# When the last group's first weight slabs are asked for, and when the sums that make them pause

## The chip, the cores and the metric

The kernel runs on one core of one Trainium2 chip. The metric is device time in microseconds (us), from the start to the end of the kernel on the device. Five engines work side by side, each in its own order: TensorE multiplies matrices (PE in the profile, its weight loads PEld), VectorE (DVE), ScalarE (ACT) and GpSimd (POOL) do elementwise work, and SyncE (SP) issues nearly all of this kernel's DMAs. [...]

## The reference

Two blocks follow each other: attention within chunks of 64 tokens, and a Fourier mix with a two-layer network behind it. All is in 32-bit floats; the two network weights come as 64-bit floats.

```
scores = q_c @ k_c.T / sqrt(64)                 # 8 batches, 8 heads, 9 chunks of 64 tokens
out    = softmax(scores) @ v_c
x      = out, heads side by side                # (8, 576, 512)
u      = x + real(fft(fft(x, axis=1), axis=2))
un     = (u - mean(u)) / sqrt(var(u) + 1e-6)    # over the last axis
result = u + relu(un @ w_ch1) @ w_ch2           # 512 -> 2048 -> 512
```

## The kernel before

**Groups and steps.** The 4,608 tokens are 36 tiles of 128 rows; four tiles are a group, and there are nine groups, numbered 0 to 8 (`NG` is 9). Group g is the four large tiles of batch g, for g up to 7; group 8 is the four tiles of "rest" rows, left over from pairs of batches. The network of a group is a Python generator, `mlp(g)`, that yields after each step. The main loop at the end of the kernel runs the generators one after the other, counts the steps in `t`, and after each step lets other work go on: attention and Fourier mix of later batches, and the weight work below. `begin[g]` is the step count at which group g begins. Group 6 begins at 182, group 7 (`NG - 2`) at 212, group 8 (`FEW`) at 242. The order of every engine's instructions is the order in which this loop writes them.

**Products.** From group 2 on, the first layer is done in `up_halves`: each pair of row blocks takes seven products instead of eight, with combined weights that were stored to DRAM in `s1`. There are four pairs, so 28 products of 16 PE instructions each (L1262). From group 1 to group 7 the second layer is done in `down_halves`, with seven products and combined weights from `s2` (L1313). In group 8 alone it is done in `down_few`, which takes 26 products for a 4 by 2 blocking (L1377); its weights are blocks from `s2` and sums of them, in `s3`.

**Slabs.** Weights are fetched by `fetch(which)`, which issues one request on SP. `fetch(1)` (L1135) brings a 256 KB slab of `s1` into one of ten places in `wa`; it is called after each up product, for the product ten later, and waits until PE has finished with the place. `fetch(2)` (L1140) brings a 1 MB slab of `s2` into one of three places in `wb`, after each of the seven down products. `fetch(3)` (L1138) brings a 512 KB slab for one of the 26 products; there are eleven places, six in the space of `wb` that `down_halves` has left, and five (`more`) in tiles that are free by then. Its first eleven requests are made by the main loop, the others by `down_few` after each product.

**Weight sums.** The blocks in `s3` are made once, by the generator `make_rest`. It works in two halves; in each it loads eight blocks (L1104), makes 23 sums or differences on POOL (L1113, `MADE`), and stores 19 of them (L1120), each store three stored sums behind the sum that was just made. It has 14 half-block buffers, so that some sums wait until an earlier store has left its buffer. It yields after every second sum, and between the loads. The main loop starts it at step 202 (`ready_at[NG - 3]`), in group 6, and steps it once a step from 207 on; it is done at step 233, in the down phase of group 7.

**Other work on POOL.** In the up phases it makes operands (L1149), in `down_halves` four sums after the second product (L1345) and parts of the output after the third and fourth (L1350, L1325, L1326); in group 8 it makes operands for `down_few` (L1163). The outputs go out on SP (L1027, L1036).

## Time and profile before

| | |
|---|---|
| median of three runs | 1081.1 us (1078.39, 1081.1, 1081.45) |
| profiled execution | 1078.96 us, span 1076.9 us |
| PE busy, PE weight loads busy | 1053.0 us (98%), 837.3 us (78%) |
| DVE, POOL, ACT busy | 585.0 us (54%), 406.1 us (38%), 310.3 us (29%) |
| DMA | 212.71 MB, mean 198 GB/s |
| granted TensorE clock | 0.998 |

All of the profile's times count from the start of the span. Group 7 runs its up products from 875.3 and its down products from 925.3, group 8 its up products from 975.3 and its 26 products from 1026.3. Rows of PE's timeline overlap a little[...]: a row's start is better for measuring pace than its length. In a row of the windows, the stretch is followed by its length, and by the busy time and number of instructions of PE, PEld, DVE, ACT and POOL; then come the granted clock, DMA's busy share, and GB/s. In a row of a timeline, start and length are followed by engine, line, operation, output and inputs, and the number of instructions; idle time before it, and what ended it, stand in brackets.

### The profile page before, as it was taken

How to read it: one execution, taken by the hardware profiler on the slowest of the kernel's cores; microseconds unless marked ns; L12 is line 12 of the kernel's file. 1: busy time of each engine (PE TensorE's matmuls, PEld its weight loads, DVE VectorE, ACT ScalarE, POOL GpSimd, SP SyncE). 2: the span in 40 equal slices, each digit the busy share in tenths (PEclk: the TensorE clock that was granted, in tenths of full speed). 3: DMA queues.
4: the chain of work that ended last, by engine and by line, in shares of the span. 5: the costliest groups of instructions: out<-in, count | busy, mean ns of one | idle time of the engine just before them, and what ended most of it. 6: DMA issues, size and time to landing. Idle time of an engine off the chain costs nothing.

```text
span 1076.9 us, 19916 instructions
## 1 busy us (share of the span) xinstructions
PE 1053.0 (98%) x7402; PEld 837.3 (78%) x7402; DVE 585.0 (54%) x1271; ACT 310.3 (29%) x730; POOL 406.1 (38%) x531
## 2 busy tenths in 40 slices
PE   8999989999999999999999999999999999999997
PEld 6645445446888888888888888888888888888786
DVE  4898985324567465664565554745564435433331
ACT  4688563212113411322032312331233012101200
POOL 4311017573515140344134321624061837850281
PEclk9999999999999999999999999999999999999999
DMA  8767466598467546883678256945653569957563
GB/s 176 240 184 214 122 190 210 162 299 292 153 193 224 161 155 181 231 238 118 189 210 229 99 183 199 260 129 189 208 158 110 196 211 317 337 174 241 186 225 107
DMA packets 159293, 212.71 MB, mean 198 GB/s; under 512 B 69308, under 2 KB 106172, under 8 KB 152926
## 3 DMA queue, kind: packets, MB, share of 16 engines
q1 hardware_dynamic: 155548, 208.04, 63.0%
q10 hardware_dynamic: 3330, 2.76, 1.1%
q8 instruction: 59, 0.97, 0.4%
q0 software_dynamic: 320, 0.66, 0.3%
q14 instruction: 36, 0.29, 0.1%
HBM read 177.31 MB, written 34.08 MB: 196 GB/s over the span
## 4 chain that ended last, share of the span: by engine, by line
PE 77%; DMA 6%; DVE 5%; issue 3%; POOL 3%; ACT 3%; SPq 3%; POOLq 0%; DVEq 0%; ACTq 0%
PE pb L1313 18%; PE pa L1262 16%; PE pa L1313 14%; PE pb L1262 12%; PE dn L1377 4%; PE up L1195 2%; PE pt L397 2%; DMA xall<-in_moe_w_ch_dram 2%; PE mix L838 2%; DMA wa<-s 2%; PE z L719 1%; PE xp L498 1%; SPq L263 1%; PE up L1175 1%; PE sc L448 1%
## 5 line engine op out<-in xcount | busy, mean ns | idle before, releaser
L1262 PE MATMUL pa<-unT,wa 128*128 128x256 f32 x672 | 159.9, 381 | 1.6 <-DVE wa L1270 1.6
L1262 PEld LDWEIGHTS pa<-unT,wa 128*128 128x128 f32 x672 | 126.3, 190 | 19.5 <-DVE wa L1270 2.1
L1262 PE MATMUL pb<-wa 128*128 128x256 f32 x448 | 106.7, 381 | 2.6 <-DMA wa<-s 2.6
L1313 PE MATMUL pa<-wb,h 128*128 128x256 f32 x448 | 101.5, 380 | 0.0
L1313 PE MATMUL pb<-wb,h 128*128 128x256 f32 x448 | 100.7, 379 | 0.0
L1262 PEld LDWEIGHTS pb<-wa 128*128 128x128 f32 x448 | 84.2, 190 | 14.8 <-issue 2.8
L1313 PEld LDWEIGHTS pa<-wb,h 128*128 128x128 f32 x448 | 83.9, 190 | 11.3
L1313 PEld LDWEIGHTS pb<-wb,h 128*128 128x128 f32 x448 | 84.1, 190 | 10.9
L1149 POOL TENSOR_TENSOR h<-h 128x256 f32<-128x256 f32 x56 | 47.0, 850 | 96.2 <-DVE wb L1147 93.4
L555 POOL COPY xall<-xall 1x512 f32<-1x512 f32 x28 | 17.8, 636 | 147.9 <-DVE xall L515 120.4
L1268 DVE TENSOR_TENSOR wa<-pb,wa 128x256 f32<-128x256 f32 x56 | 23.7, 424 | 73.0 <-ACT wa L1267 73.0
L1216 PE MATMUL dn<-wb,h 128*128 128x512 f32 x128 | 58.9, 609 | 0.0
L1267 ACT COPY wa<-pa 128x256 f32<-128x256 f32 x56 | 20.8, 372 | 126.8 <-PE pa L1262 126.8
L1195 PE MATMUL up<-unT,wa 128*128 128x512 f32 x128 | 56.8, 596 | 0.0
L1262 PE MATMUL pa<-wa 128*128 128x256 f32 x224 | 53.9, 384 | 0.8 <-DMA wa<-s 0.8
L1262 PE MATMUL pb<-unT,wa 128*128 128x256 f32 x224 | 53.0, 379 | 0.0
L1313 PE MATMUL pb<-wb,yall 128*128 128x256 f32 x224 | 51.2, 382 | 0.0
L1313 PE MATMUL pb<-wb 128*128 128x256 f32 x224 | 50.7, 379 | 0.0
L1313 PE MATMUL pa<-wb,yall 128*128 128x256 f32 x224 | 50.5, 379 | 0.0
L1276 ACT ACTIVATE h<-pa 128x256 f32<-128x256 f32 x56 | 21.5, 383 | 100.7 <-PE pa L1262 99.8
L1175 PE MATMUL up<-unT,wa 128*128 128x512 f32 x108 | 49.4, 598 | 0.0
L1262 PEld LDWEIGHTS pa<-wa 128*128 128x128 f32 x224 | 41.7, 190 | 7.2 <-ACT wa L1267 1.1
(287 smaller groups left out, 1955.7 us busy)
## 6 DMA issues: line engine op xcount, KB each, us to landing
wb<-s SPq DMA_DIRECT2D x49, 1024.0 KB
wa<-s SPq DMA_DIRECT2D x196, 256.0 KB
xall<-in_moe_w_ch_dram SPq DMA_DIRECT2D x22, 512.0 KB
q<-in_q_dram SPq DMA_DIRECT2D x96, 112.0 KB
k<-in_k_dram SPq DMA_DIRECT2D x96, 112.0 KB
wb<-s SPq DMA_DIRECT2D x16, 512.0 KB
v<-in_v_dram SPq DMA_DIRECT2D x124, 64.0 KB
s<-part SPq DMA_DIRECT2D x30, 256.0 KB
```

The lines of the kernel that those rows point to most:

```text
L397: nc.tensor.transpose(pt[:, j, :], src(j), ident)
L838: nc.tensor.matmul(out=mix[:, cols], lhsT=zt[:, T], rhs=tab, start=(T == 0), stop=(T == 3), skip_group_check=True,)
L1149: nc.gpsimd.tensor_tensor(out=h1[:, m, hi], in0=h1[:, m, lo], in1=h1[:, m, hi], op=ALU.subtract)
L1175: nc.tensor.matmul(out=up, lhsT=w1[:, kk, m * 128:(m + 1) * 128], rhs=unT[:, kk], start=(kk == 0), stop=(kk == KD - 1), skip_group_check=True,
L1195: nc.tensor.matmul(out=up, lhsT=w1[:, kk, m * 128:(m + 1) * 128], rhs=unT[:, kk], start=(kk == 0), stop=(kk == KD - 1),)
L1216: nc.tensor.matmul(out=dn, lhsT=h1[:, m, s * 128:(s + 1) * 128], rhs=w2[:, m, :], start=(m == 0), stop=(m == KF - 1),)
L1262: nc.tensor.matmul(out=dst, lhsT=w[:, kk, r], rhs=rhs[o][:, kk], start=(o in (0, 1) and kk == 0), stop=(kk == 1), skip_group_check=True,)
L1267: nc.scalar.copy(a, dst)
L1268: nc.vector.tensor_tensor(out=b, in0=pbs[r][:, 0], in1=a, op=ALU.add)
L1276: nc.scalar.activation(out=h1[:, m, lo], in_=dst, func=ACTF.Relu)
L1313: nc.tensor.matmul(out=dst, lhsT=lhs[:, m], rhs=w[:, m], start=(o in (0, 2) and m == 0), stop=(m == HF - 1), skip_group_check=True,)
L1377: nc.tensor.matmul(out=dst, lhsT=lhs[:, m], rhs=w[:, m], start=(fresh and not half and m == 0), stop=(m == 3), skip_group_check=True,)
```

## The change

Two places in the main loop change. `make_rest` is no longer stepped at steps 215, 219, 223, 227, 231, 235 and 239, that is, at every fourth step from the beginning of group 7; its 28 stretches end at step 240 instead of 233. The eleven first `fetch(3)` requests of group 8 are no longer all made at step 244, but one at each of the steps 244 to 254; the places for them are set up at step 244 as before.

```diff
                 if t == ready_at[NG - 3]:
                     rest_ = make_rest()
                     next(rest_)
-                if t > ready_at[NG - 3] + 4:
+                if t > ready_at[NG - 3] + 4 and (t < begin[NG - 2] or t % 4 != 3):
                     next(rest_, None)
                 if t == begin[FEW] + 2:
                     more = [xall[:, 2 * G:2 * G + 4, :].rearrange("p a f -> p (a f)")[:, i * Z3:(i + 1) * Z3] for i in range(2)]
                     more += [one_p.tile([128, Z3], FP32, tag=tag, name="more") for tag in ("q", "k", "zf")]
                     slab3.extend(a.rearrange("p (m e) -> p m e", m=4) for a in more)
-                    for _ in range(NS3):
-                        fetch(3)
+                if begin[FEW] + 2 <= t < begin[FEW] + 2 + NS3:
+                    fetch(3)
```

The SP requests of that stretch are the same in number and size, in another order. TensorE, VectorE and ScalarE have the same instructions in the same order as before; on POOL, sums of `make_rest` stand later among its other work.

## The prediction

> **What bounds the kernel now.** I read the page first (PE busy 98% of the span, weight loads 78%, the next engine 54%), then PE's waits, the windows of the last two groups, PE's timeline there, the DMA queue's timeline, and POOL's waits. TensorE is the bound, at full granted clock, so a change gains only where PE stands still. The windows are the up and down phases of group 7, then those of group 8:

> ```profile
> 875.28:925.33 50.05, 49.05 (x226) 42.33 (x225) 24.87 (x52) 13.55 (x31) 34.07 (x29) 1.00 0.89 307
> 925.33:975.28 49.95, 49.95 (x241) 43.99 (x241) 15.80 (x30) 2.45 (x6) 31.29 (x29) 1.00 0.61 205
> 975.28:1026.26 50.98, 48.59 (x226) 42.49 (x225) 16.95 (x40) 13.73 (x31) 7.84 (x7) 1.00 0.61 216
> 1026.26:1076.90 50.64, 45.04 (x209) 39.34 (x207) 12.51 (x31) 0.69 (x2) 27.00 (x22) 1.00 0.55 177
> ```

> Length first, then PE's busy time: the two up phases hold 1.00 and 2.39 us of idle PE, the down phases none before the tail. PE's timeline shows where:

> ```profile
> 909.65 1.89 PE L1262 MATMUL pa<-unT,wa 128*128 128x256 f32 x8
> 911.77 1.97 PE L1262 MATMUL pb<-wa 128*128 128x256 f32 x8 [0.23 <-DMA wa<-s]
> 913.57 1.89 PE L1262 MATMUL pa<-unT,wa 128*128 128x256 f32 x8
> 916.23 1.97 PE L1262 MATMUL pa<-wa 128*128 128x256 f32 x8 [0.77 <-DMA wa<-s]
> ...
> 997.71 1.89 PE L1262 MATMUL pa<-unT,wa 128*128 128x256 f32 x8
> 1002.00 1.97 PE L1262 MATMUL pb<-wa 128*128 128x256 f32 x8 [2.39 <-DMA wa<-s]
> ```

> A row is one up product, with one 256 KB slab. From 975.27 to 997.71 thirteen of them start 1.726 us apart; 28 make 48.3 us. Against that pace group 7 loses 1.7 us and group 8 2.7 us: **4.4 us is all there is to gain**. The DMA queue shows why the slabs are late. In group 8:

> ```profile
> 977.19 5.50 SPq L1135 DMA_DIRECT2D wa<-s  x4
> 982.74 3.86 SPq L1138 DMA_DIRECT2D wb<-s  x6
> 986.65 1.21 SPq L1138 DMA_DIRECT2D xall<-s  x2
> 988.13 2.87 SPq L1138 DMA_DIRECT2D more<-s  x3
> 991.97 12.35 SPq L1135 DMA_DIRECT2D wa<-s  x11
> ```

> Eleven 512 KB requests (5.77 MB) stand ahead of the fifth up slab. It is asked for at 991.97 and, by the chain of work, takes 9.89 us: the very slab that PE waits for until 1002.00. DMA moved 402 GB/s from 986 to 996. In group 7 it is the weight sums' stores and loads:

> ```profile
> 898.80 0.90 SPq L1135 DMA_DIRECT2D wa<-s  x2
> 899.81 5.52 SPq L1120 DMA_DIRECT2D s<-part  x4
> 905.42 0.88 SPq L1104 DMA_DIRECT2D part<-s  x2
> 906.41 1.89 SPq L1135 DMA_DIRECT2D wa<-s  x2
> 908.65 0.32 SPq L1104 DMA_DIRECT2D part<-s  x1
> 909.03 0.42 SPq L1104 DMA_DIRECT2D xall<-s  x1
> 909.55 0.44 SPq L1135 DMA_DIRECT2D wa<-s  x1
> ```

> The row at 898.80 ends with the 11th slab request of group 7. Four stores then hold the queue 5.5 us: the last waits for the first half's last sum (POOL, 903.71 to 904.98). So the 12th and 14th requests go out at 906.41 and 909.55, and PE waits for these two, 0.23 and 0.77 us.

> [...]

> **The change part by part.** PE, DVE and ACT have the same instructions in the same order. POOL and SP have the same work reordered.

> *Part 1, one slab a step.* The 11 requests go out at the end of group 8's steps 2 to 12 instead of all at step 2. No byte and no instruction is added. Between two of them now stand one or two up slabs, each tied to PE's pace (3.45 us a step of two products). Demand: 18 up slabs of 256 KB and 11 of 512 KB are 10.5 MB over 48.3 us, 217 GB/s, half of what the burst reached. An up slab then has at most one 512 KB request just ahead, 1.3 us at 402 GB/s; it is requested ten products, 17.3 us, before its use. Even with the slowest landing seen, 9.89 us, it comes in time. Gain: 2.7 us. The other side is lateness: with both stalls gone group 8 starts at 973.6, its 12th step ends 21 products, 36.3 us, later at 1009.9, where the 11th product slab is asked for; its product runs at 973.6 + 48.3 + 10 x 1.73 = 1039.2. That is a cover of 29 us against a landing of 1.3 us (its bytes at 402 GB/s) to 9.9 us (the slowest seen): nothing.

> *Part 2, the pause.* From step 0 of group 7 (212 in the step count) the sums skip every fourth step: they end at step 240 instead of 233, before group 8 starts (242). POOL's sums are 1.30 us each (mean of L1113), 23 in each half. For group 7's up phase: before, 11 slab requests stand ahead of the four stores; after, 14 do. From 887.03 to 899.81 the queue passed 19 requests, 0.67 us each. Counting the new order from the same store at 887.03, the 12th slab request is 19 places on, 899.8, and the 14th 901.1, instead of 906.41 and 909.55. With 6.55 us to land (the chain's figure for the late one) they are there at 906.4 and 907.7; PE wants them at 875.28 + 21 x 1.726 = 911.5 and at 915.0. The next in danger, the 15th, now stands behind the four stores and two loads: sums end about 905, so it goes at 906.3, lands at 912.9, and is wanted at 916.7. The 17th goes where the 14th went, 909.55, lands at 916.1, wanted at 920.2. All have 3.8 us to spare. Gain: 1.7 us. From the 19th on the slabs are for group 8, 50 us away.

> *Where the pushed work goes.* Ten more sums than before fall behind POOL's four L1345 sums of the down phase. These come sooner or at the same time; they wait for PE's second down product, 923.6 + 2 x 6.91 = 937.4, and end at 942.7 (before: 948.8, behind the backlog). Then four sums to 947.9, then L1350 to 949.3 (before: 954.0), which shortens DVE's 5.63 us wait for L1350. The other L1113 sums fit in between and end near 964, with the last four stores behind them. Those stand between group 7's output stores on SP; the ones behind wait for DVE until about 968 anyway, and group 8's first slab request waits for PE at 975.3. On SP, the 1 MB down slabs now have stores ahead of them that wait for POOL: the third one goes when PE releases the buffer at 944.4, its stores needing only a sum ended at 944; before it went at 953.09, behind five stores. The fourth waits for PE at 951.3. No cost.

> *Sum.* -2.7 - 1.7 = -4.4 us at most. [...] I take **-4.2 us**. On the profiled execution (1078.96 us, of which the span is 1076.9): 1074.8, a ratio of 0.9961. That execution lies 0.2% below the median of the runs; the ratio on 1081.1 gives 1076.9.

> **Rivals.**
> 1. *Only the burst's stall goes*, because in group 7 DMA stays full (0.89 busy) and another slab is late in place of the two: the 15th's 3.8 us of slack is the thinnest place. For it: landings there took 5 to 6.6 us and sums could run later than before. Against: three more slab requests are ahead, 5.2 us of PE's work. -2.7 + 0.2: 1078.6.
> 2. *Nothing moves*: the slabs that come late in group 8 are just other ones, or group 7's gain is lost again at the first down slab. Against: 217 GB/s, and 29 us of cover. 1081.
> 3. *Slower*, by a ring between SP and POOL in group 7's down phase: POOL waits for a buffer whose store stands behind a 1 MB request, SP holds this until PE frees its slab, and the third such request stands behind stores of sums not yet made. The trace of before shows the kind: POOL waited 15.53 us for a store, until 875.14, while SP waited for PE's down slabs. The third slab is wanted at 923.6 + 5 x 6.91 = 958.2; 1 MB needs 2.6 us at 402 GB/s and at most 6.7 (asked for at 953.09, used at 959.8), so a request after 951.5 stops PE: POOL has 7 us to lose. A wait of 15.5 us there makes PE late by 8.5, net +4.3: 1085.4. It decides from 11.3 us on. Against: the one sum that needs a store behind such a request (the 13th, its store at about 931) comes after L1345, which holds POOL until 942.7 anyway.

> **How the numbers follow.** A difference under 0.3% (3.2 us) is about what a measurement of this kernel can't tell from none: its three runs span 3.06 us. The forecast -4.2 has 0.62; rival 1 0.19; rival 2 0.08; rival 3 0.11. The forecast lands beyond -0.3% some 8 times in 10 (0.50), rival 1 2 in 10 (0.04): faster 0.54. The rest of these and rival 2 make same 0.35; slower 0.11. Low end: the profiled execution's level less all of 4.4, 1074.5. High end: rival 2 at the highest run, 1081.5. Outside lie rival 3 and some 0.06 of noise. The likeliest case's own range is 1075.4 to 1078.4 (half the runs' spread each way).

> **What would show it.** Right: no PE wait for wa in either up phase, both near 48.3 us; no 400 GB/s stretch in group 8's up phase; L1138 requests single, about 3.5 us apart; sums running on past L1350 to about 964; down phases as long as before. Wrong: a PE wait for wb in group 7's down phase (rival 3), for wa after 911 (rival 1), or for dn's slabs after 1022.

## The result and the profile after

The changed kernel takes 1077.22 us (median of 20 runs, 1074.83 to 1080.25), the kernel before 1080.18 us (20 runs, 1076.95 to 1081.64): ratio 0.9976, with an interval of 0.9967 to 0.9986. That is 2.6 us, inside the predicted range, and a little less than the 0.3% beyond which the prediction counted it as faster. Two repeats further down gave 0.9962 and 0.9969.

The profiled execution took 1076.13 us, its span 1074.1 us. The windows of the changed kernel, again for the up and down phases of group 7 and of group 8 (length, then busy time of PE, PEld, DVE, ACT and POOL, granted clock, DMA share, GB/s):

```profile
876.53:924.89 48.36, 48.36 (x226) 42.59 (x225) 24.13 (x52) 13.57 (x31) 31.05 (x27) 1.00 0.90 318
924.89:975.18 50.29, 50.27 (x241) 44.05 (x241) 18.10 (x30) 2.45 (x6) 34.90 (x31) 1.00 0.62 195
975.18:1023.54 48.36, 48.36 (x226) 42.59 (x225) 16.95 (x40) 13.89 (x31) 8.00 (x7) 1.00 0.65 236
1023.54:1074.10 50.56, 44.90 (x209) 39.20 (x207) 12.51 (x31) 0.54 (x2) 26.85 (x22) 0.97 0.54 177
```

Both up phases are at PE's own pace: 48.36 us with no idle time, where they took 50.05 and 50.98. From first product to first product, group 7's down phase is 0.2 us longer (50.31 against 50.11); the 0.2 us stand in front of one transpose (L397), and the profile does not show what ended that wait. From the start of group 7 to the end of the span the two profiles differ by 4.1 us. They differ by only 2.8 us in the whole span, because this execution came to group 7 1.26 us later (876.38 against 875.12), in a part of the program in which the change has moved nothing.

The DMA queue's timeline of the changed kernel, first where group 7's slabs were late, then at group 8's requests:

```profile
900.61 1.62 SPq L1135 DMA_DIRECT2D wa<-s  x3
902.54 4.04 SPq L1120 DMA_DIRECT2D s<-part  x4
907.00 0.81 SPq L1104 DMA_DIRECT2D part<-s  x2
907.91 0.85 SPq L1135 DMA_DIRECT2D wa<-s  x2
...
989.04 2.05 SPq L1135 DMA_DIRECT2D wa<-s  x2
991.14 0.42 SPq L1138 DMA_DIRECT2D wb<-s  x1
992.50 2.05 SPq L1135 DMA_DIRECT2D wa<-s  x2
994.59 0.42 SPq L1138 DMA_DIRECT2D wb<-s  x1
```

The row at 900.61 holds the 12th to 14th slab requests, now ahead of the four stores. Group 8's product slabs go out one at a time between up slabs, except the last three, which go together at 1006.68. DMA still has a full stretch there, fuller and longer than the 402 GB/s over 10 us of the old burst:

```profile
992.00:1007.00 15.00, 15.00 (x72) 13.20 (x71) 5.58 (x14) 3.61 (x8) 7.48 (x6) 1.00 1.03 409
```

No slab comes late in it: by the updates of the DMA semaphores in the trace, each up slab that group 8 asks for lands at least 5.8 us before its product is due. But one stretch looks worse than before. These are the same queue's last requests of group 7:

```profile
966.15 1.10 SPq L1027 DMA_DIRECT2D out_dram<-wb  x2
968.85 0.81 SPq L1036 DMA_DIRECT2D out_dram<-wb  x2
969.75 5.90 SPq L1120 DMA_DIRECT2D s<-part  x4
975.74 1.08 SPq L1027 DMA_DIRECT2D out_dram<-wb  x2
976.92 1.96 SPq L1036 DMA_DIRECT2D out_dram<-wb  x2
978.98 6.95 SPq L1135 DMA_DIRECT2D wa<-s  x4
985.98 0.42 SPq L1138 DMA_DIRECT2D wb<-s  x1
```

The four last stores of the sums take 5.90 us of the queue, the output stores behind them are late, and group 8's first slab is asked for 3.9 us after the group begins, where it was 1.9 before (977.19 against 975.27). No PE wait comes of it here. What it is worth without the other half of the change is the main finding of the experiments.

### The profile page after: what moved, and what is told of

It reads as the page before. It is cut to its first block, busy times and chain, and to the rows that moved or that the text cites. A ratio compares the mean times of both kernels' runs of the same rounds, so it can differ in the third digit from the quotient of the medians.

```text
span 1074.1 us, 19924 instructions
## 1 busy us (share of the span) xinstructions
PE 1052.4 (98%) x7402; PEld 838.0 (78%) x7402; DVE 586.5 (55%) x1271; ACT 310.6 (29%) x730; POOL 406.8 (38%) x531
## 4 chain that ended last, share of the span: by engine, by line
PE 82%; DMA 5%; DVE 5%; ACT 3%; SPq 3%; issue 1%; POOL 0%; DVEq 0%; ACTq 0%
PE pb L1313 18%; PE pa L1262 18%; PE pa L1313 14%; PE pb L1262 13%; PE dn L1377 4%; PE up L1195 4%; PE pt L397 2%; PE dn L1216 2%; DMA xall<-in_moe_w_ch_dram 2%; PE mix L838 2%; PE z L719 1%; PE xp L498 1%; PE sc L448 1%; SPq L263 1%; DMA out_dram<-o 1%
## 5 line engine op out<-in xcount | busy, mean ns | idle before, releaser
L1262 PE MATMUL pa<-unT,wa 128*128 128x256 f32 x672 | 160.0, 381 | 1.5 <-DVE wa L1270 1.5
L1262 PEld LDWEIGHTS pa<-unT,wa 128*128 128x128 f32 x672 | 126.3, 190 | 19.3 <-DVE wa L1270 2.0
L1262 PE MATMUL pb<-wa 128*128 128x256 f32 x448 | 106.6, 381 | 0.0
L1262 PEld LDWEIGHTS pb<-wa 128*128 128x128 f32 x448 | 84.4, 190 | 11.5
L1262 PE MATMUL pa<-wa 128*128 128x256 f32 x224 | 53.9, 383 | 0.0
L1262 PE MATMUL pb<-unT,wa 128*128 128x256 f32 x224 | 52.9, 379 | 0.0
L1313 PE MATMUL pa<-wb,yall 128*128 128x256 f32 x224 | 50.5, 379 | 0.0
L1175 PE MATMUL up<-unT,wa 128*128 128x512 f32 x108 | 49.4, 598 | 0.0
L855 POOL TENSOR_TENSOR xall<-y,xall 128x513 f32<-128x513 f32 x14 | 21.4, 1526 | 68.4 <-DVE y L849 68.4
```

What stands on the lines that cost most here:

```text
L855: eng.tensor_tensor(out=x[:, 0:w], in0=y[:, 0:w], in1=x[:, 0:w], op=ALU.add)
L1175: nc.tensor.matmul(out=up, lhsT=w1[:, kk, m * 128:(m + 1) * 128], rhs=unT[:, kk], start=(kk == 0), stop=(kk == KD - 1), skip_group_check=True,
L1262: nc.tensor.matmul(out=dst, lhsT=w[:, kk, r], rhs=rhs[o][:, kk], start=(o in (0, 1) and kk == 0), stop=(kk == 1), skip_group_check=True,)
L1313: nc.tensor.matmul(out=dst, lhsT=lhs[:, m], rhs=w[:, m], start=(o in (0, 2) and m == 0), stop=(m == HF - 1), skip_group_check=True,)
```

## The experiments

The theory: what counts is the order of requests on SP. A slab is late when something that waits, or something large, stands ahead of it. In the kernel before, the four stores ahead of group 7's late slabs held the queue 5.5 us (the last waited for a sum that ended at 904.98), the burst ahead of group 8's 9.2 us. Rivals: the change works by moving bytes out of a full stretch; the pause costs something by itself; only one of the two parts does the work.

The table has every run, with the time that the two up phases lost against 48.35 us (the pace), worked out from the starts of the phases' first products on PE's timeline. "Group 8 asks" is the time from the start of the group to its first slab request.

| run | ratio to before, interval | group 7 up lost | group 8 up lost | group 8 asks |
|---|---|---|---|---|
| before, first profile | | 1.70 | 2.63 | 1.9 |
| again_before | 0.9997, 0.9985 to 1.0010 | 1.01 | 4.44 | 1.9 |
| the change, first profile | 0.9976, 0.9967 to 0.9986 | 0 | 0 | 3.9 |
| again_after | 0.9962, 0.9950 to 0.9975 | 0 | 0 | 3.8 |
| after_third | 0.9969, 0.9956 to 0.9983 | 0 | 0 | 3.5 |
| spread_only | 0.9969, 0.9959 to 0.9979 | 1.05 | 0 | 1.9 |
| spread_again | 0.9970, 0.9959 to 0.9981 | 0.33 | 0 | 1.9 |
| pause_only | 1.0045, 1.0026 to 1.0064 | 0.68 | 8.36 | 4.1 |
| pause_no_tail | 0.9997, 0.9983 to 1.0012 | 0 | 4.28 | 1.9 |
| one_pause | 0.9997, 0.9983 to 1.0012 | 0.15 | 4.50 | 1.9 |
| burst_later | 0.9994, 0.9980 to 1.0007 | 0.26 | 1.46 | 1.9 |
| late_burst | 0.9956, 0.9940 to 0.9973 | 0 | 0 | 4.0 |
| one_pause_spread | 0.9964, 0.9951 to 0.9977 | 0 | 0 | 1.9 |
| late_spread | 0.9965, 0.9953 to 0.9976 | 0.48 | 0 | 3.5 |

### Each part alone, and both kernels once more

Part 1 alone is this edit of the kernel before:

```diff
-                    for _ in range(NS3):
-                        fetch(3)
+                if begin[FEW] + 2 <= t < begin[FEW] + 2 + NS3:
+                    fetch(3)
```

> Part 1 alone. Theory: the up slabs of group 8 come in time and nothing else changes: group 8's up phase 48.4 us instead of 51.0, group 7's still about 50 us with PE waits of about 1 us for wa; 2.6 us less than before (-0.24%). Rival, that the whole gain comes from one part: 4.2 us less here and nothing from the pause alone, or the other way round.

As the theory had it: group 8's up phase 48.35 us, group 7's still with a wait for wa, and 0.9969. The gain is 3.4 us where 2.6 was expected; the interval of the ratio, 2.3 to 4.4 us, holds both. The PE timeline's row for group 7's wait, in this kernel:

```profile
916.80 1.97 PE L1262 MATMUL pb<-wa 128*128 128x256 f32 x8 [0.81 <-DMA wa<-s]
```

Part 2 alone:

```diff
-                if t > ready_at[NG - 3] + 4:
+                if t > ready_at[NG - 3] + 4 and (t < begin[NG - 2] or t % 4 != 3):
                     next(rest_, None)
```

> Part 2 alone. Theory: group 7's up phase 48.4 us instead of 50.05, the burst's wait in group 8 stays at 2.4 us; about 1.6 us less than before (-0.15%). Rival, that stores pushed into the down phase cost as much there: group 7's down phase longer than 49.95 us, no gain.

Neither theory nor rival: it is 0.45% (4.9 us) slower than before. The down phase is not to blame (50.24 us, against 50.1); the loss is in group 8's up phase. The DMA queue and PE's timeline of this kernel, and its windows around the wait:

```profile
975.18 5.90 SPq L1120 DMA_DIRECT2D s<-part  x4
981.17 1.09 SPq L1027 DMA_DIRECT2D out_dram<-wb  x2
982.35 2.08 SPq L1036 DMA_DIRECT2D out_dram<-wb  x2
984.52 6.62 SPq L1135 DMA_DIRECT2D wa<-s  x4
991.20 4.08 SPq L1138 DMA_DIRECT2D wb<-s  x6
```
```profile
1002.91 1.89 PE L1262 MATMUL pa<-unT,wa 128*128 128x256 f32 x8
1010.37 3.75 PE L1262 MATMUL pb<-wa 128*128 128x256 f32 x8 [5.57 <-DMA wa<-s]
1013.91 2.70 PE L1262 MATMUL pa<-unT,wa 128*128 128x256 f32 x8
```
```profile
1000.00:1008.00 8.00, 4.80 (x23) 3.88 (x21) 1.78 (x5) 2.86 (x6) 3.65 (x3) 1.00 1.02 418
1008.00:1016.00 8.00, 5.63 (x14) 4.59 (x15) 0.00 (x0) 0.21 (x1) 3.81 (x4) 0.57 0.94 360
```

Two things are added to the old wait. The burst starts 10.7 us after group 8 begins (991.20 against 980.46) instead of 7.5, with the same four slabs ahead of it, and so PE waits 3.2 us longer, 5.57 us. And the product after the wait takes 3.75 us instead of 1.89: the granted clock was 0.57 in that stretch.

> The kernel before, once more. If the two waits for slabs are fixed by the order of requests, this profile shows them again within 0.3 us (1.7 us lost in group 7's up phase, 2.6 in group 8's), and only the stretch before group 7 differs from the first profile, by up to 1.5 us. If they depend on chance, one of them is smaller here, and the mean gain of the change is smaller than the 4.2 us that the first pair of profiles shows from group 7 on. Ratio 1.000.

The waits are there again, but not within 0.3 us. Group 7 loses 1.01 us (one slab late instead of two), and group 8 4.44, of which the wait is 2.52. PE's timeline and the windows of this second profile show the rest:

```profile
1005.39 3.16 PE L1262 MATMUL pb<-wa 128*128 128x256 f32 x8 [2.52 <-DMA wa<-s]
1008.34 2.43 PE L1262 MATMUL pa<-unT,wa 128*128 128x256 f32 x8
```
```profile
1006.00:1009.00 3.00, 3.00 (x9) 2.38 (x8) 0.00 (x0) 0.00 (x0) 2.92 (x4) 0.50 1.03 395
```

For some 3 us behind the wait PE ran at half clock. The first profile of the same kernel does not have this (its row after the wait takes 1.97 us).

> The changed kernel, once more. If the 1.3 us by which the first profile of it came late at group 7 is chance, this one starts group 7 somewhere between 874.5 and 876.5 and again has both up phases at 48.4 us. If it belongs to the change, group 7 starts about 1.3 us later than in the kernel before again. Ratio 0.996 by the first, 0.9975 by the second.

Both up phases 48.35 us, as expected, and 0.9962. Group 7 began at 879.46, outside the 874.5 to 876.5 that I gave for chance, but so it did in the kernel before (879.06): the late start belongs to the execution, not to the change. Over all profiles group 7 begins between 873.4 and 881.2. The stretch before it, which no edit here changes, so varies more than the change is worth.

### Why the pause alone is slower

```diff
+                if t > ready_at[NG - 3] + 4 and (t < begin[NG - 2] or t % 4 != 3):
                     next(rest_, None)
+                if t == begin[FEW] - 5:
+                    for _ in rest_:
+                        pass
```

> The pause alone, as in pause_only, but what is left of the sums after step 237 is written out at once, so that their last stores stand ahead of group 7's output stores and not between them; the burst of eleven requests stays. Theory (the pause alone was slower because the four stores between the output stores made group 8's first up slabs and with them the burst 3 us later): the first up slab of group 8 is asked for about 2 us after the group begins, as before, not 3.9; PE waits 2.4 us for a slab, not 5.6; in all about 1 us faster than before. Rival (the pause itself costs, through POOL or the memory): group 8's wait stays above 4 us, and it is slower than before by some 4 us.

The queue's timeline of this kernel:

```profile
957.67 8.01 SPq L1120 DMA_DIRECT2D s<-part  x5
966.77 1.10 SPq L1027 DMA_DIRECT2D out_dram<-wb  x2
969.47 0.81 SPq L1036 DMA_DIRECT2D out_dram<-wb  x2
972.85 1.08 SPq L1027 DMA_DIRECT2D out_dram<-wb  x2
976.38 0.79 SPq L1036 DMA_DIRECT2D out_dram<-wb  x2
977.57 5.50 SPq L1135 DMA_DIRECT2D wa<-s  x4
983.12 1.88 SPq L1138 DMA_DIRECT2D wb<-s  x4
```

With the stores ahead of the output stores, where the queue was waiting for DVE in any case, group 8 asks after 1.9 us, the burst starts after 7.5, and PE waits 2.45 us instead of 5.57. All pauses but the last are still there, and so is group 7's gain. So the four stores between the output stores are shown to be what made the pause slower. The total is 0.9997 and not the 1 us gained that I expected; the interval holds both. Half clock followed the wait here too (the granted clock was 0.97 over the phase, against 1.00 before), and group 8 lost 4.28 us. What held the four stores is seen in part in the waits of the changed kernel's DMA queue, from 964 to 987 (us in total, number of waits, longest): two of the four stores, and two slab requests behind them, waited for output stores to land.

```profile
SPq L1135 <- DMA out_dram<-wb: 4.3, 2, 3.6
SPq L1120 <- DMA out_dram<-wb: 2.4, 2, 2.1
```

In the changed kernel's trace the 895 requests of the queue use eight semaphores, mostly in turn (752 have the semaphore of the request eight places before), and each of the last four stores went out behind the last update of the request before it on its semaphore. The third and fourth of the stores started at 972.44 and 975.33; the output stores before them on their semaphores, asked for at 966.15 and 966.73, had sent their last updates at 972.38 and 975.26. These two waits are 2.4 of the 5.90 us. The row of the second store is 1.69 us long, for a reason that the profile does not show.

### Order or bytes

```diff
-                if t > ready_at[NG - 3] + 4:
+                if t > ready_at[NG - 3] + 4 and t != begin[NG - 2] + 6:
```

> One pause only, at step 218 (in front of the first half's last stores and the second half's loads); the burst stays. By the queue's order, the 12th and 13th slabs of group 7 go out ahead of the four stores, and the wait in group 7 is gone: up phase 48.4 to 48.6 us. By the bandwidth rival (the pauses help because bytes leave the full up phase), moving the same bytes by one step changes little: 49.4 to 50 us as before. Group 8's wait stays at 2.4 to 2.6 us in both; total 0 to 1.7 us faster than before.

One pause, in front of the four stores, takes group 7's wait away: 48.5 us, no wait for a slab. Its DMA queue's timeline has the four slab requests, the 10th to 13th, ahead of the stores:

```profile
902.35 3.10 SPq L1135 DMA_DIRECT2D wa<-s  x4
905.54 3.31 SPq L1120 DMA_DIRECT2D s<-part  x4
908.96 0.89 SPq L1104 DMA_DIRECT2D part<-s  x2
```

DMA was as busy in that up phase as before (0.90, 319 GB/s, by the windows, against 0.89, 307). This speaks for order and against the rival of bytes, and so does the changed kernel, whose group 8 loses nothing in 15 us at 409 GB/s. The test in group 7 is not as sharp as I meant it: unpaused kernels lost as little as 0.26 us there (burst_later) and as much as 1.70. Group 8's wait was 2.58 us, and the total, 0.9997, lies at the low end of what was expected.

> The kernel before with its burst at step 246 instead of 244, nothing else. Two steps bring four more up slabs ahead of it and start it 6.9 us later, so by the queue's order both sides move alike: the wait in group 8 stays, 2.4 to 3 us, now in front of product 18 or 19 instead of 15. If it were the time of the burst that counts, the wait would grow to 9 us or vanish. Total as before within 0.1%.

The edit puts the burst under `if t == begin[FEW] + 4:`. Half right. The total is as before and the wait is in front of the 18th product, but it is 1.23 us, not 2.4 to 3:

```profile
1006.59 1.96 PE L1262 MATMUL pb<-unT,wa 128*128 128x256 f32 x8 [1.23 <-DMA wa<-s]
```

My count was off: the two steps hold three products, so the burst moved by 5.2 us (12.7 against 7.5) and three more slabs stood ahead. Both sides did move alike. The rest, 1.2 us, is that this burst held the queue 8.5 us instead of 9.2, and that the slab behind it landed 0.5 us sooner. The time of the burst as such is not what counts: the wait neither vanished nor grew to 9 us. This profile lost 1.7 us in the two up phases, where those of the kernel before lost 4.3 and 5.5, and yet the ratio is 0.9994. The profiled execution was 1.8 us faster than the median of its own runs: one profile does not price a wait.

```diff
+                if t == begin[FEW] + 11:
+                    for _ in range(NS3):
+                        fetch(3)
```

> The changed kernel with all eleven requests at once at step 253, after the last up slab has been asked for. Queue theory: a burst harms only what stands behind it, so no wait in group 8's up phase (48.4 us), and the first of its slabs has 17 us to land: total as the changed kernel, -3 to -4.5 us against before. Rival (the burst harms by filling the DMA engines, whatever stands behind it): waits for the last up slabs, or for the first product slabs, of 2 us or more.

This edit is made to the changed kernel, in place of its one request a step. The queue's timeline:

```profile
999.78 3.77 SPq L1135 DMA_DIRECT2D wa<-s  x3
1003.61 3.63 SPq L1138 DMA_DIRECT2D wb<-s  x6
1007.28 0.96 SPq L1138 DMA_DIRECT2D xall<-s  x2
1008.35 3.81 SPq L1138 DMA_DIRECT2D more<-s  x3
```

The same eleven requests in one burst, behind the last up slab: no wait anywhere, 0.9956. Here the burst did no harm that can be seen; ahead of up slabs, in the kernel before, it left PE waiting 2.39 us for the slab behind it.

### What the pause adds, and how much cover there is

> The changed kernel, a third time, beside spread_again on the same chip: both up phases 48.35 us; ratio to before between 0.996 and 0.9975.

> Part 1 alone again, to see what the pause adds to it. If the pause adds what is lost in group 7's up phase (0.3 to 1.7 us in the four profiles that have no pause), this is 0.03 to 0.16% slower than after_third, and its profile shows a wait for wa in group 7. If the pause adds nothing, both ratios are equal within 0.05%.

On one chip, 0.9969 and 0.9970. I had expected spread_again's profile to name a wait for wa in group 7. It names none: it puts a wait of 0.5 us down to DVE. But the wait stands in front of the 22nd product, whose slab was late in the kernel before too, and by the semaphores that slab landed at 911.07, just before its weights were loaded at 911.17; DVE had finished at 910.77. The five profiles without a pause lost 0.87 us on average in group 7's up phase; the seven with all pauses (in pause_no_tail all but the last) lost 0.17, but had a down phase 0.2 us longer on average (50.1 to 50.5 against 50.1). The pause is thus worth some half a microsecond on top of part 1, too little for the totals to show: by the totals alone, part 1 does all the work, and what the pause adds stands on the profiles. In pause_only and late_spread, group 7 lost time earlier in the phase, when no slab was late: weight loads waited for DVE instead (L1272 and L1281, 0.4 us each in late_spread; L1272 alone, 0.18 us of PE, in pause_only).

> One pause at step 218 with one request a step: if the seven pauses are worth no more than the one in front of the first half's last stores, both up phases are 48.4 to 48.5 us, the first up slab of group 8 is asked for 1.9 us after the group begins instead of 3.9, and the time is that of after_third. If the other pauses matter, group 7 has a wait for wa or a down phase above 50.3 us.

As expected: no wait in either phase, the down phase at 50.1, and group 8's first request at 1.9 us.

> The changed kernel with the eleven requests at steps 248 to 258 instead of 244 to 254. The prediction gave them 29 us of cover, so four steps (13.8 us) more cost nothing: both up phases 48.35 us, no wait for a product slab, ratio as after_third. If the cover were under 14 us, PE would wait at the first of the 26 products or at the eleventh.

No wait for a product slab, group 8 at 48.35 us: the cover is more than 13.8 us. Group 7 was 0.48 us off, for the reason just given.

late_burst and one_pause_spread are the fastest by their medians (1076.16 and 1076.27 us), but their intervals overlap that of the changed kernel, so no version here is shown to beat it.

## Why the prediction was right, and where not

**The bound and the gap.** Right. PE was the limit, the two up phases held what could be gained, and both now run at the pace that was worked out from PE's rows (48.3 us).

**Part 1.** Right that the burst's place in the queue made the wait; the reason given for why spreading would help was only half right. I had reckoned with a demand of 217 GB/s and taken "no 400 GB/s stretch in group 8's up phase" for a sign of being right. That sign did not come: DMA moved 409 GB/s for 15 us, and the slabs were in time because they had been asked for early enough. It was order and not quantity (late_burst shows the same). The 2.7 us were the price of one profile whose wait was followed by full clock. In three other profiles with the burst at the same place (again_before, pause_no_tail, one_pause) the phase lost 4.3 to 4.5 us, because half clock followed (a granted clock of 0.97 over the phase in all three). The mean of the four is 4.0; the measured part 1 is 3.3 us on average, with intervals from 2.1 to 4.4 that leave room for 2.7.

**Part 2.** Its working for group 7 held closely. Shifted by the 1.26 us of the late start, the 12th slab was to be asked for at 901.1, the 15th at 907.6; they were asked for at 900.6 and 907.9, and the 15th landed 3.8 us before its product was due, the very slack that was worked out. The size did not hold. The 1.7 us again came from one profile, the largest of five, and the mean is 0.87.

**Where the pushed work goes.** This is the step that failed: "No cost" for the four last stores on SP. I had worked out that their sums end in time (near 964; they ended at 964.7, though the L1345 sums began 2.4 us sooner than worked out, before PE had ended its second down product) and that the output stores behind them wait for DVE anyway. I had not asked how long the stores themselves would hold the queue. They held it 5.90 us, 2.4 of them in waits of two stores for earlier output stores to land. The term put at nothing could have been priced: where group 7 begins, the kernel before has stores of sums behind output stores too, and the waits of its DMA queue (from 876 to 930) show two of them held for 5.2 us.

```profile
SPq L1120 <- DMA out_dram<-wb: 5.2, 2, 2.7
```

In the changed kernel this hides behind the ten slabs fetched ahead, since the burst is gone; with the burst in place it costs 4.9 us. So the sum of two independent gains was wrong too: the parts are -3.3 and +4.9 us alone, and -3.3 together (0.9969, the mean of three ratios).

**The rivals.** Rival 1 (only group 8's wait goes) came nearest in the first ratio, 0.9977 against 0.9976, but not in cause: both waits went, and so rival 2 (nothing moves) fell too. Rival 3 looked for the harm of pushed stores in group 7's down phase, where the third 1 MB slab was asked for at 946.1 against the 944.4 worked out, far from the limit. The harm was later on the queue, at the entrance of group 8.

**The total.** The forecast was 4.2 us, of the 4.4 to be gained; the 0.2 us between them were my estimate. The first comparison gave 2.6, the repeats 4.1 and 3.4, with a mean of 3.3. The median of 1077.22 lies close to the 1076.9 given, partly because the kernel before was measured 0.9 us below the three runs that the forecast started from; so close a hit is luck.

## What to carry to other kernels

For each DMA request, ask which later request on the same queue is needed first: a prefetch that is issued too early does harm if it stands ahead of something needed sooner, as the eleven requests did here (9.2 us of the queue, and a PE wait of 2.39 us). When stores are moved, count how long each will hold the queue until an earlier DMA has landed, not only when its data is ready (for the four stores here 2.4 of 5.90 us). And price a short wait from several profiles: one here varied from 0.3 to 1.7 us in kernels with the same code in that stretch.

## What the hardware showed that I had not expected

Cut along its trace's grid, the wait shows how the first profile differed. These are windows of before, one_pause and again_before, two of each: the stretch that holds most of the wait, and the next.

```profile
998.08:1001.50 3.42, 1.52 (x8) 0.99 (x6) 1.11 (x3) 1.52 (x4) 2.34 (x2) 1.00 1.01 381
1001.50:1004.91 3.41, 2.91 (x14) 2.61 (x15) 0.00 (x0) 0.05 (x1) 3.33 (x4) 1.00 1.05 403
1001.85:1005.26 3.41, 1.39 (x7) 1.26 (x8) 0.00 (x0) 0.42 (x1) 3.33 (x4) 1.00 1.05 404
1005.26:1008.67 3.41, 3.41 (x10) 2.69 (x9) 0.24 (x1) 0.37 (x1) 3.05 (x3) 0.50 1.01 380
1002.59:1006.00 3.41, 0.89 (x5) 0.59 (x4) 0.43 (x1) 0.81 (x2) 3.33 (x3) 1.00 1.02 388
1006.00:1009.41 3.41, 3.41 (x10) 2.70 (x9) 0.00 (x0) 0.00 (x0) 3.33 (x4) 0.50 0.99 379
```

Length less PE's busy time is 1.90 us of idle PE in before, 2.02 in one_pause and 2.52 in again_before; it is 2.28 in pause_no_tail and 1.22 in burst_later. Where it was 2.02 us or more, the next stretch had half clock; where it was 1.90 or less, it had not. So PE was not idle throughout the stretch ahead of half clock (in one_pause it was busy for 1.39 of 3.41 us), and how much of a wait fell into one stretch depended on where it lay on the grid: that of before was cut into 1.90 us and 0.50 us. Two profiles show the like elsewhere. In before, half clock followed 2.05 us of idle PE (154.99 to 158.41) and did not follow 1.88 us (1069.76 to 1073.17); in the changed kernel it followed 2.06 us (156.23 to 159.64) and 2.56 us (1067.59 to 1071.00). So few stretches do not show where a limit lies, or that there is a fixed one.

Three of four need not be the typical share. Worked out from the granted clock of every run, with all that is missing from 1 taken as time at 0.50, the kernel before spent 5.8 us a run at half clock on average (170 runs), and the kernels without a wait in group 8 5.0 us (143 runs). The difference, 0.8 us with an interval of 0.1 to 1.5, is about a quarter of one stretch of 3.41 us: perhaps one execution in four paid it. This is an estimate, and it fits a part 1 of 3.3 us better than the 4.0 of the four profiles.
